# Two-stage weight conversion, a later GpSimd product, and other PSUM banks for the first and last batch

## The chip, the cores and the metric

The kernel runs on one core of a Trainium2 chip. The metric is the device time of one execution in microseconds (us). The engines are TensorE (PE; its weight loads are listed apart as PEld), VectorE (DVE), ScalarE (ACT), GpSimd (POOL), and SyncE (SP), which only issues DMAs here. Every engine works through its own queue in order.

## The reference, cut to what matters

Three blocks follow one another, for B = 8 batches, S = 576 tokens and width 512:

```python
# 1. retention: 8 heads of 64
scores = scale * q @ k.T
ret = scores * Dmat          # causal decay gamma ** (i - j)
x = (ret @ v)                # -> (B, S, 512)
# 2. four attention experts, two of them chosen per token
logits = x @ w_gate
for e in range(4):
    q, k, v = x @ wq[e], x @ wk[e], x @ wv[e]
    a = softmax(causal(scale * q @ k.T))
    out += weight_of_token_for_e * (a @ v @ wo[e])
# 3. mixing of tokens, then of channels
theta = x @ w_theta
zr, zi = x * cos(theta), x * sin(theta)
u = x + w_tok_r @ zr + w_tok_i @ zi
out = u + relu(u @ w_ch)
```

All inputs are float32. The weights of the third block reach the kernel as 64-bit floating-point numbers, seen as pairs of 32-bit words.

## The kernel before, in words

A large matmul is made of three: each operand is split into a high part and a low part (`split`, an ACT copy and a subtraction), and high by high, low by high and high by low are added in PSUM (`mm3`).

**First half, up to about 484 us.** Block 1 and block 2 are interleaved. A loop over 80 units (batch, pair of experts, row chunk) writes attention scores, transposes and products; a list of slots says in which unit a chunk of the next batch goes through retention (`ret_step`, a "visit") and which projections are made. The order on PE is the order of the code (`manual_schedule`); on the other engines a scheduler sets it, by its own estimate of when operands are ready. At a visit of chunk c, `ret_values` makes `xt`, ACT its high part `xh`, GpSimd its low part `xl` (L183), and the projections (L98 to L100, L242) then wait for both. The same visit loads chunk c+3 (`loads`: `kt` L114, `kv` L117) and has GpSimd multiply its values by decay factors (`vp`, L119). `vp` has three buffers, as have the loads.

Beside this, 51 jobs convert the 64-bit weights of block 3: a load (`raw`, L426), five operations on DVE (L433 to L439), an ACT copy of the low words (`r`, L441), GpSimd's `r*ex` (L442), an ACT copy for the high part (`h`, written to `hl`, L443), and GpSimd's `d = v-h` and `l = d+r` (L445, L446). All are written one behind the other in one job; the result goes back to DRAM with the next job (L453). The temporaries have one buffer each.

**Second half.** For each batch, `mix(b, h)` for h = 0, 1 (each 9 steps of contraction, two blocks of 128 channels, token columns in two pieces `TS` = 256 and 320) writes four PSUM banks `acc00` to `acc11`; DVE moves them to `u` (L723, for batch 0 L725), ACT and GpSimd or DVE split `u` (L726, L727). Then `channel` makes four blocks of 128 channels in the four banks named `w`, again in pieces of 256 and 320, and DVE evicts each (L740). The operands of `mix` come from `z_tile`: DVE takes |theta| (L564), subtracts pi/2 (L565), clamps (L566), ACT takes the sine of both halves at once (L567), DVE multiplies by x (L569), ACT and DVE split (L103, L104). `load_o` fetches attention outputs and token weights (`og`, one buffer, L519) and multiplies them on GpSimd (L520); `x_put` and `x_get` carry x, transposed by DVE (L751), through DRAM to the next batches' `u`.

Of the kernel before, what the change touches and what calls it, by code (L numbers as in the profile page):

```python
# [10 lines left out]
F32 = mybir.dt.float32  # L11
F32R = mybir.dt.float32r
# [48 lines left out]
def tile_kernel(ctx: ExitStack, tc: tile.TileContext, qk, kv, w1, wo, wot, wd, cst, out):  # L61
# [45 lines left out]
    MARK = {}  # L107
    QKT, KVT, XT, PSS, VP, SM, PX = {}, {}, {}, {}, {}, {}, {}

    def loads(b, c):  # L110
        R = ROWS[c]
        o = c * 1024
        t = ret.tile([128, 8, R], F32, name="kt", bufs=LDB, padded_shape=[128, 8, 128])
        nc.sync.dma_start(t, qk[b, :, o:o + 8 * R].rearrange("p (h r) -> p h r", h=8))  # L114
        n = R // 64
        u = ret.tile([128, 2, 2, 256], F32, name="kv", bufs=LDB)
        nc.sync.dma_start(u[:, :n], kv[b, c, :, :n * 512].rearrange("r (j a d) -> r j a d", j=n, a=2))  # L117
        vp = ret.tile([128, 2, 4, D], F32, name="vp", bufs=VPB)
        MARK["pool"] = nc.gpsimd.tensor_mul(vp[:, :n], u[:, :n, 1, :].rearrange("p j (h d) -> p j h d", h=4),  # L119
                                            gam[:, c, :n, :, None].to_broadcast([128, n, 4, D]))  # L120
        QKT[b, c], KVT[b, c], VP[b, c] = t, u, vp

# [300 lines left out]
    def convert(cvt, h, l, src, n):  # L423

        raw = cvt.tile([128, n, 2], I32, name="raw", bufs=2, padded_shape=[128, CV, 2])
        nc.sync.dma_start(raw, src.bitcast(I32).rearrange("p (n t) -> p n t", t=2))  # L426
        lo, hi = raw[:, :, 0], raw[:, :, 1]

        def tmp(name, dt):
            return cvt.tile([128, n], dt, name=name, bufs=1, padded_shape=[128, CV])  # L430

        b1 = tmp("b1", I32)
        nc.vector.tensor_scalar(b1, hi, 3, 0x3FFFFFF8, op0=OP.logical_shift_left, op1=OP.bitwise_and)  # L433
        nc.vector.scalar_tensor_tensor(b1, hi, -0x40000000, b1, op0=OP.bitwise_and, op1=OP.bitwise_or)
        ex = tmp("ex", I32)
        nc.vector.tensor_scalar(ex, hi, 0x7FF00000, None, op0=OP.bitwise_and)
        v = b1.bitcast(F32)
        nc.vector.scalar_tensor_tensor(v, ex, float(0x38100000), v, op0=OP.is_ge, op1=OP.mult)
        nc.vector.tensor_scalar(ex, b1, -0x800000, None, op0=OP.bitwise_and)  # L439
        r = tmp("r", F32)  # L440
        nc.scalar.activation(r, lo.bitcast(U32), AF.Copy, scale=2.0 ** -52)  # L441
        nc.gpsimd.tensor_mul(r, r, ex.bitcast(F32))  # L442
        nc.scalar.activation(h, v, AF.Copy)  # L443
        d = tmp("d", F32)
        nc.gpsimd.tensor_sub(d, v, h)  # L445
        nc.gpsimd.tensor_add(l, d, r)  # L446

    PEND = []

    def flush():  # L450
        while PEND:
            dst, t = PEND.pop()
            nc.sync.dma_start(dst, t)  # L453

    def cvt_jobs(pl, weights):

        def job(dst, off, o, n):
            t = pl.tile([128, 2, n], F32R, name="hl", bufs=2, padded_shape=[128, 2, CV])
            convert(pl, t[:, 0, :], t[:, 1, :], wd[:, off + o:off + o + n], n)
            flush()  # L460
            PEND.append((dst[:, :, o:o + n], t.bitcast(F32)))

        return [lambda a=(dst, off, x, min(CV, w - x)): job(*a) for dst, off, w in weights for x in range(0, w, CV)] + [flush]

# [48 lines left out]
    def load_o(b):  # L513
# [43 lines left out]
    def z_tile(g, i, h):  # L557
# [116 lines left out]
    def mix(b, h):  # L674
        g, w = divmod(b, 2)
        tiles = [0, 1, 2, 3, 4] if w == 0 else [4, 5, 6, 7, 8]
        acc = [[ps2.tile([128, t1 - t0], F32, name=f"acc{d}{i}", bufs=1, padded_shape=[128, 512])
                for i, (t0, t1) in enumerate(TS)] for d in range(2)]
        ks = []
# [48 lines left out]

    TAIL = {}

    def channel(b, et):
        uh, ul = UT[b]
        u = XU[b]
        es = slice(et * C, et * C + C)
        for t0, t1 in TS:
            ps = ps2.tile([128, t1 - t0], F32, name="w", bufs=4, padded_shape=[128, 512])
            for kt in range(4):
                mm3(ps, CH[:, kt, 0, es], CH[:, kt, 1, es], uh[:, kt, t0:t1], ul[:, kt, t0:t1], kt == 0, kt == 3)
            o = u[:, et, t0:t1]
            nc.vector.scalar_tensor_tensor(o, ps, 0.0, o, op0=OP.max, op1=OP.add)  # L740
            if b == B - 1:
# [31 lines left out]
    for b in range(B):  # L773
# [103 lines left out]
```

## Time and profile before

| | |
|---|---|
| median of 3 runs | 912.73 us (907.61 to 915.47) |
| profiled execution | 907.77 us, its span 905.8 us |
| busy in the span | PE 863.0 us (95%), PEld 803.9, DVE 628.8 (69%), ACT 454.9 (50%), POOL 218.9 (24%) |
| mean granted clock of TensorE | 0.992 |

A time is in us from the span's start. Matmuls are pipelined: the listed time of one is longer than the distance from its start to the next one's, and that distance is what a matmul costs PE. A number in square brackets at the end of a row is the idle time of the engine just before, with the instruction whose end released it.

### The profile page before, as it was taken

The numbers are of one execution on the slowest core, as the hardware profiler recorded it, in microseconds if no ns is written. First come the engines' busy times: TensorE is split into PE (matmuls) and PEld (weight loads), VectorE is DVE, ScalarE is ACT, GpSimd is POOL, SyncE is SP. The second block draws the span as 40 slices with busy tenths as digits, with TensorE's granted clock in tenths as the row PEclk, the third lists the DMA queues.
The fourth block names the chain that finished last, engine by engine and source line by source line (L and its number), as shares of the span: only waits on it lengthen the run. The fifth ranks groups of instructions, "written<-read, shape, count | busy, mean of one in ns | idle before, by whom it ended". The sixth has DMA issues, their size and how long they took to land.

```text
span 905.8 us, 25503 instructions
## 1 busy us (share of the span) xinstructions
PE 863.0 (95%) x10062; PEld 803.9 (89%) x10062; DVE 628.8 (69%) x1779; ACT 454.9 (50%) x1198; POOL 218.9 (24%) x268
## 2 busy tenths in 40 slices
PE   6998999899999999998999989999999999999998
PEld 6987888788898888888878889999999999999998
DVE  5376767878787776777769947866578764676732
ACT  2466666666666665665656513443244533434320
POOL 2434152452535434242212102001020110001010
PEclk8999999999999999999999999999999999999999
DMA  7857566676667667656795152333425123251401
GB/s 276 237 143 234 159 203 170 187 223 184 194 182 241 167 180 227 163 148 207 202 317 173 30 143 50 62 90 92 128 50 135 35 72 80 37 125 25 106 23 53
DMA packets 146216, 130.30 MB, mean 144 GB/s; under 512 B 83504, under 2 KB 121648, under 8 KB 146096
## 3 DMA queue, kind: packets, MB, share of 16 engines
q1 hardware_dynamic: 145952, 128.39, 50.1%
q8 instruction: 79, 1.29, 0.6%
q0 software_dynamic: 144, 0.28, 0.2%
q14 instruction: 41, 0.34, 0.1%
HBM read 78.03 MB, written 32.00 MB: 121 GB/s over the span
## 4 chain that ended last, share of the span: by engine, by line
PE 67%; DVE 10%; DMA 8%; ACT 6%; issue 3%; POOL 2%; SPq 2%; DVEq 0%; ACTq 0%; POOLq 0%
PE acc L711 22%; PE w L99 9%; PE w L98 9%; PE w L100 9%; PE w L242 4%; PE w L370 4%; PE w L304 3%; DMA kv<-kv 3%; PE w L351 2%; ACT P L312 2%; PE pS L150 2%; DVE P L307 1%; DMA TK<-td 1%; DMA wst<-w 1%; ACT U L225 1%
## 5 line engine op out<-in xcount | busy, mean ns | idle before, releaser
L711 PE MATMUL acc<-TK,zh 128*128 128x256 f32 (+1 forms) x1024 | 180.7, 299 | 3.4 <-ACT zh L103 1.8
L711 PEld LDWEIGHTS acc<-TK,zh 128*128 128x128 f32 x1024 | 155.7, 191 | 4.0 <-issue 3.7
L312 ACT ACTIVATE P<-P,st 128x128 f32<-128x128 f32 (+4 forms) x160 | 95.6, 598 | 55.9 <-DVE st L307 55.5
L711 PE MATMUL acc<-TK,zl 128*128 128x256 f32 (+1 forms) x512 | 110.9, 298 | 0.0
L727 POOL TENSOR_TENSOR ul<-u,uh 128x576 fp32r<-128x576 f32 x16 | 24.3, 1540 | 336.4 <-ACT uh L726 336.4
L307 DVE CUSTOM_DVE_ANT_0 P<-w,cm 128x128 f32<-128x128 f32 (+4 forms) x160 | 71.8, 477 | 24.4 <-PE w L304 24.1
L711 PEld LDWEIGHTS acc<-TK,zl 128*128 128x128 f32 x512 | 87.0, 191 | 0.0
L103 ACT ACTIVATE zh<-cs 128x512 fp32r<-128x512 f32 x64 | 40.4, 631 | 90.2 <-PE acc L711 68.2
L99 PE MATMUL w<-xl,WH 128*128 128x288 f32 x256 | 75.9, 296 | 4.5 <-POOL xl L183 4.5
L567 ACT ACTIVATE cs<-cs 128x512 f32<-128x512 f32 x72 | 45.2, 631 | 69.1 <-DVE cs L565 55.2
L98 PE MATMUL w<-uh,CH 128*128 128x256 f32 (+1 forms) x256 | 75.5, 297 | 2.4 <-ACT uh L726 2.4
L98 PE MATMUL w<-xh,WH 128*128 128x288 f32 x256 | 76.0, 297 | 0.7 <-ACT PT L356 0.7
L104 DVE TENSOR_TENSOR zl<-cs,zh 128x512 fp32r<-128x512 f32 x64 | 44.0, 690 | 46.4 <-ACT zh L103 45.7
L304 PE MATMUL w<-KK,U 128*64 128x288 f32 (+4 forms) x384 | 76.2, 327 | 0.0
L99 PE MATMUL w<-ul,CH 128*128 128x256 f32 (+1 forms) x256 | 75.7, 296 | 0.0
L100 PE MATMUL w<-uh,CH 128*128 128x256 f32 (+1 forms) x256 | 75.6, 296 | 0.0
L100 PE MATMUL w<-xh,WL 128*128 128x288 f32 x256 | 75.4, 295 | 0.0
L150 PE MATMUL pS<-vp,kv 64*64 64x64 f32 x1024 | 44.0, 226 | 19.8 <-ACT S L153 15.9
L442 POOL TENSOR_TENSOR r<-r,ex 128x192 f32<-128x192 f32 (+1 forms) x51 | 29.5, 579 | 136.4 <-ACT hl L443 61.8
L569 DVE SCALAR_TENSOR_TENSOR cs<-cs,x 128x512 f32<-128x512 f32 x72 | 48.7, 687 | 18.6 <-ACT cs L567 18.4
L304 PEld LDWEIGHTS w<-KK,U 128*128 128x128 f32 (+1 forms) x384 | 53.9, 171 | 7.5 <-issue 4.3
L150 PEld LDWEIGHTS pS<-vp,kv 64*64 64x64 f32 x1024 | 35.8, 137 | 27.1 <-ACT S L153 18.5
(140 smaller groups left out, 2267.2 us busy)
## 6 DMA issues: line engine op xcount, KB each, us to landing
KK<-KN SPq DMA_DIRECT2D x128, 144.0 KB
kt<-qk SPq DMA_DIRECT2D x32, 512.0 KB
kv<-kv SPq DMA_DIRECT2D x32, 512.0 KB
raw<-wd SPq DMA_DIRECT2D x43, 192.0 KB
xd<-xb SPq DMA_DIRECT2D x126, 64.0 KB
out<-u SPq DMA_DIRECT2D x28, 288.0 KB
u<-xd SPq DMA_DIRECT2D x28, 288.0 KB
td<-hl SPq DMA_DIRECT2D x27, 192.0 KB
```

The costliest lines, as they stand in the source:

```text
L98: nc.tensor.matmul(ps, ah, bh, start=first, stop=False)
L99: nc.tensor.matmul(ps, ah, bl, start=False, stop=False)
L100: nc.tensor.matmul(ps, al, bh, start=False, stop=last)
L103: nc.scalar.activation(h, src, AF.Copy)
L104: nc.vector.tensor_sub(l, src, h)
L150: nc.tensor.matmul(pS[half(s), x, :], u[half(s), j, 0, x * D:x * D + D], vp[half(s), j, x, :], start=k == 0 and x == 0, stop=False, skip_g ...
L304: nc.tensor.matmul(ps[s][:R], U[:, s, rs], KK[:, s, x, j0:j1], start=x == 0, stop=x == 1)
L307: MARK["dve"] = nc.vector.tensor_tensor_reduce(Ps[s][:R, j0:j1], ps[s][:R], cm[:R, o + j0:o + j1], 1.0, st[:R, 0, s:s + 1] if i else 3.0e3 ...
L312: MARK["act"] = nc.scalar.activation(Ps[s][:R, :n], Ps[s][:R, :n], AF.Exp, bias=st[:R, last, s:s + 1], scale=-1.0, accum_out=SUM[p][:R, m, ...
L567: nc.scalar.activation(cs, cs, AF.Sin)
L569: nc.vector.scalar_tensor_tensor(z, cs, -1.0, x2[:, None, ds].to_broadcast([128, 2, 256]), op0=OP.mult, op1=OP.mult)
L711: nc.tensor.matmul(acc[d][j], A[:, dc], TK[:, kt, W, t0:t1], start=q == 0 and n == 0, stop=q == 8 and n == 2)
```

## The change

1. **Conversion in two stages.** A job now first finishes the job before it (GpSimd's `r*ex`, ACT's `h`, GpSimd's `v-h`, in place, and the sum), and then does its own load, the five DVE operations and ACT's `r`. The temporaries have two buffers, and a result is stored one job later.
2. **GpSimd's product later.** `loads` only notes the chunk; `scale`, at the end of the next visit, makes `vp`.
3. **Banks for the edge batches.** For b = 0 and 7, `mix(b, 1)` accumulates in the four `w` banks, and `channel` of these batches in the `acc` banks.
4. **Pieces of 288.** Batches 1 to 7 in `mix` and all batches in `channel` use 288 and 288 columns for 256 and 320.
5. **pi/2 as a bias.** DVE's subtraction goes; ACT takes the sine in two instructions of 256, one with a bias.
6. **`load_o`'s product** waits for the last `channel` eviction written before it, if there is one.
7. **Batch 0's `x_put`s** are written behind the channel blocks, `x_get(1)` at the end.

```diff
     def loads(b, c):
...
-        vp = ret.tile([128, 2, 4, D], F32, name="vp", bufs=VPB)
-        MARK["pool"] = nc.gpsimd.tensor_mul(vp[:, :n], u[:, :n, 1, :].rearrange("p j (h d) -> p j h d", h=4),
-                                            gam[:, c, :n, :, None].to_broadcast([128, n, 4, D]))
-        QKT[b, c], KVT[b, c], VP[b, c] = t, u, vp
+        QKT[b, c], KVT[b, c] = t, u
+        RAW.append((b, c))
+
+    def scale_v(b, c):
+        n = ROWS[c] // 64
+        vp = VP[b, c] = ret.tile([128, 2, 4, D], F32, name="vp", bufs=VPB)
+        MARK["pool"] = nc.gpsimd.tensor_mul(vp[:, :n], KVT[b, c][:, :n, 1, :].rearrange("p j (h d) -> p j h d", h=4),
+                             gam[:, c, :n, :, None].to_broadcast([128, n, 4, D]))
+
+    def scale():
+        if RAW:
+            scale_v(*RAW.pop(0))
@@ -198,6 +209,8 @@
+        if (b, c) > (0, 1):
+            scale()
@@ -439,28 +455,42 @@
-        nc.gpsimd.tensor_mul(r, r, ex.bitcast(F32))
-        nc.scalar.activation(h, v, AF.Copy)
-        d = tmp("d", F32)
-        nc.gpsimd.tensor_sub(d, v, h)
-        nc.gpsimd.tensor_add(l, d, r)
...
+        def rest():
+            nc.gpsimd.tensor_mul(r, r, ex.bitcast(F32))
+            nc.scalar.activation(h(), v, AF.Copy)
+            nc.gpsimd.tensor_sub(v, v, h())
+            nc.gpsimd.tensor_add(l(), v, r)
...
+    def finish():
+        flush()
+        if REST:
+            rest, pl, n, dst = REST.pop()
+            t = pl.tile([128, 2, n], F32R, name="hl", bufs=2, padded_shape=[128, 2, CV])
+            HL[:] = [t]
+            rest()
+            PEND.append((dst, t.bitcast(F32)))
...
         def job(dst, off, o, n):
...
+            finish()
+            rest = convert(pl, lambda: HL[0][:, 0, :], lambda: HL[0][:, 1, :], wd[:, off + o:off + o + n], n)
+            REST.append((rest, pl, n, dst[:, :, o:o + n]))
@@ -517,7 +549,10 @@
-        nc.gpsimd.tensor_mul(OL[b], OL[b], gw)
+        m = nc.gpsimd.tensor_mul(OL[b], OL[b], gw)
+        if "ch" in MARK:
+            tc.add_manual_dep(m.ins, MARK["ch"].ins.name, mybir.DependencyInfo(
+                mybir.DependencyClass.Sync, mybir.DependencyReason.DATA), reason="behind the channel products")
@@ -562,9 +597,9 @@
-        nc.vector.tensor_scalar(cs[:, 0, :], cs[:, 0, :], math.pi / 2.0, None, op0=OP.subtract)
         nc.vector.tensor_scalar(cs[:, 1, :], nr[:, ds], PI_LO, -PI_LO, op0=OP.min, op1=OP.max)
-        nc.scalar.activation(cs, cs, AF.Sin)
+        nc.scalar.activation(cs[:, 0, :], cs[:, 0, :], AF.Sin, bias=quarter)
+        nc.scalar.activation(cs[:, 1, :], cs[:, 1, :], AF.Sin)
@@ -674,8 +709,10 @@
-        acc = [[ps2.tile([128, t1 - t0], F32, name=f"acc{d}{i}", bufs=1, padded_shape=[128, 512])
-                for i, (t0, t1) in enumerate(TS)] for d in range(2)]
+        ts = TH if b else TS
+        spare = h and b in EDGE
+        acc = [[ps2.tile([128, t1 - t0], F32, name="w" if spare else f"acc{d}{i}", bufs=4 if spare else 1,
+                         padded_shape=[128, 512]) for i, (t0, t1) in enumerate(ts)] for d in range(2)]
@@ -727,17 +764,20 @@
+    EDGE = (0, B - 1)
...
-        for t0, t1 in TS:
-            ps = ps2.tile([128, t1 - t0], F32, name="w", bufs=4, padded_shape=[128, 512])
+        for j, (t0, t1) in enumerate(TH):
+            spare = b in EDGE
+            ps = ps2.tile([128, t1 - t0], F32, name=f"acc{et % 2}{j}" if spare else "w", bufs=1 if spare else 4,
+                          padded_shape=[128, 512])
```

**How the order changes on GpSimd**, at the first visits of the second batch. `xl_1008` there is the low part of that batch; `kv_1015` is loaded at the visit that makes `xt_1009`. Before:

```order
29 L446 TENSOR_TENSOR hl_1039<-d_1053,r_1049 128x192
30 L119 TENSOR_TENSOR vp_1017<-kv_1015,gam_121 128x512
31 L183 TENSOR_TENSOR xl_1008<-xt_1009,xh_1007 128x4x128
32 L442 TENSOR_TENSOR r_1189<-r_1189,ex_1185 128x192
33 L445 TENSOR_TENSOR d_1193<-b1_1182,hl_1179 128x192
34 L446 TENSOR_TENSOR hl_1179<-d_1193,r_1189 128x192
```

After:

```order
27 L460 TENSOR_TENSOR r_1048<-r_1048,ex_1044 128x192
28 L127 TENSOR_TENSOR vp_1171<-kv_1015,gam_123 128x512
29 L194 TENSOR_TENSOR xl_1008<-xt_1009,xh_1007 128x4x128
30 L462 TENSOR_TENSOR b1_1041<-b1_1041,hl_1173 128x192
31 L460 TENSOR_TENSOR r_1187<-r_1187,ex_1183 128x192
32 L463 TENSOR_TENSOR hl_1173<-b1_1041,r_1048 128x192
```

The product of `kv_1015` still stands right ahead of the same `xl`; what moved is the conversion: a job's difference and sum now stand behind `xl`, with the next job's `r*ex` between them.

**On SyncE**, in the second batch, behind the small stores of token weights (`gd`). Before:

```order
33 L326 DMA gd_93<-nwt 5x2x32 x4
34 L114 DMA kt<-qk 128x8x64
35 L117 DMA kv<-kv 128x1024
36 L453 DMA tt_81<-hl 256x1x192
37 L117 DMA kv<-kv 128x1024
38 L114 DMA kt<-qk 128x1024
```

After:

```order
31 L339 DMA gd_93<-nwt 5x2x32 x4
32 L120 DMA kv<-kv 128x1024
33 L117 DMA kt<-qk 128x8x64
34 L472 DMA tt_81<-hl 256x1x192
35 L442 DMA raw<-wd 128x384
36 L120 DMA kv<-kv 128x1024
```

The first `kv` load has passed the `kt` load.

**On DVE**, where the first half ends. `nr_8921` before and `nr_8872` after read `pS`, a bank of the first half's PSUM pool, which must be free before `mix(0, 0)` can start. Before:

```order
1104 L550 TENSOR_SCALAR k_8877<-k_8877 128x512
1105 L552 TENSOR_TENSOR nr_8880<-k_8877,w_8868 128x512
1106 L104 TENSOR_TENSOR zl_8943<-cs_8936,zh_8942 128x512
1107 L569 SCALAR_TENSOR_TENSOR cs_8946<-cs_8946,x2_8563 128x512
1108 L550 TENSOR_SCALAR k_8918<-k_8918 128x512
1109 L564 TENSOR_SCALAR cs_8975<-nr_8609 128x256
1110 L552 TENSOR_TENSOR nr_8921<-k_8918,pS_8909 128x512
```

After:

```order
1102 L585 TENSOR_SCALAR k_8828<-k_8828 128x512
1103 L587 TENSOR_TENSOR nr_8831<-k_8828,w_8819 128x512
1104 L604 SCALAR_TENSOR_TENSOR cs_8887<-cs_8887,x2_8475 128x512
1105 L585 TENSOR_SCALAR k_8869<-k_8869 128x512
1106 L587 TENSOR_TENSOR nr_8872<-k_8869,pS_8860 128x512
1107 L107 TENSOR_TENSOR zl_8894<-cs_8887,zh_8893 128x512
```

The subtraction that frees the bank has moved ahead of a low part and of a second product of `z_tile`.

## Rows read from the trace of the kernel before

**Rows 1.** Waits of PE: who was waited for, us in total, times, longest.

```profile
PE pS L150 <- ACT S L153: 15.9, 19, 2.6
PE w L99 <- POOL xl L183: 4.5, 5, 1.9
...
PE w L242 <- POOL xl L183: 1.7, 1, 1.7
```

**Rows 2.** Timeline of SP and POOL, 133 to 144 us: start, duration, instruction.

```profile
133.06 3.35 SPq L220 DMA_DIRECT2D KK<-KN  x4
...
137.09 0.44 SPq L117 DMA_DIRECT2D kv<-kv  x1
...
143.23 1.04 POOL L119 TENSOR_TENSOR vp<-kv,gam 128x512 f32<-128x512 f32 x1 [3.11 <-DMA kv<-kv]
```

**Rows 3.** Timeline of SP and POOL, 67 to 74 us.

```profile
67.71 0.34 SPq L117 DMA_DIRECT2D kv<-kv  x1
...
73.46 1.04 POOL L119 TENSOR_TENSOR vp<-kv,gam 128x512 f32<-128x512 f32 x1 [6.04 <-DMA kv<-kv]
```

**Rows 4.** Timeline of DVE, ACT and PE, 176 to 180 us.

```profile
176.06 1.43 DVE L434 SCALAR_TENSOR_TENSOR b<-raw,b 128x192 int32<-128x192 int32 x1
...
177.92 0.36 ACT L443 ACTIVATE hl<-b 128x192 fp32r<-128x192 f32 x1 [1.26 <-DVE b L438]
...
178.86 0.39 ACT L153 ACTIVATE S<-pS 128x256 f32<-128x256 f32 x1
...
179.30 0.27 PE L150 MATMUL pS<-vp,kv 64*64 64x64 f32 x2 [2.12 <-ACT S L153]
```

**Rows 5.** Timeline of POOL, DVE and PE, 475 to 486 us.

```profile
475.01 2.68 POOL L520 TENSOR_TENSOR ol<-ol,og 128x1152 f32<-128x1152 f32 x1 [17.46 <-DMA og<-gd]
...
475.60 2.24 DVE L564 TENSOR_SCALAR cs<-nr 128x256 int32<-128x256 int32 x1
...
483.88 0.68 DVE L552 TENSOR_TENSOR nr<-k,pS 128x512 f32<-128x512 f32 x1
...
484.76 1.20 PE L711 MATMUL acc<-TK,zh 128*128 128x256 f32 x4 [1.79 <-ACT zh L103]
```

**Rows 6.** Busy time by stretch: stretch, its length, each engine, granted clock, DMA.

```profile
484.00:486.00 2.00, 1.24 (x6) 1.27 (x7) 2.00 (x7) 0.78 (x2) 0.00 (x0) 0.72 0.67 204
486.00:489.50 3.50, 3.50 (x20) 3.48 (x20) 3.19 (x7) 2.12 (x4) 0.00 (x0) 0.67 0.84 230
```

**Rows 7.** Timeline of DVE and PE, 491 to 524 us and near 874 us.

```profile
491.05 2.18 DVE L564 TENSOR_SCALAR cs<-nr 128x256 int32<-128x256 int32 x1
...
521.72 1.54 DVE L725 COPY u<-acc 128x256 f32<-128x256 f32 x4
...
503.91 0.47 PE L711 MATMUL acc<-TK,zh 128*128 128x256 f32 x2 [1.63 <-DVE u L725]
...
519.73 0.28 PE L98 MATMUL w<-uh,CH 128*128 128x256 f32 x1
...
523.30 0.39 PE L98 MATMUL w<-uh,CH 128*128 128x256 f32 x1 [2.40 <-ACT uh L726]
...
874.54 0.51 PE L711 MATMUL acc<-TK,zth 128*128 128x256 f32 x2 [1.52 <-DVE u L723]
```

**Rows 8.** Groups: DVE's in 485 to 521.7 us; ACT's of the whole span.

```profile
L565 DVE TENSOR_SCALAR cs<-cs 128x256 f32<-128x256 f32 x13 | 3.7, 285 | 0.0
...
L567 ACT ACTIVATE cs<-cs 128x512 f32<-128x512 f32 x72 | 45.2, 631 | 69.1 <-DVE cs L565 55.2
```

**Rows 9.** Timeline of PE: a stretch of `mix`, and one of projections.

```profile
760.31 0.70 PE L711 MATMUL acc<-TK,zh 128*128 128x256 f32 x4
...
764.31 0.70 PE L711 MATMUL acc<-TK,zh 128*128 128x256 f32 x4
...
76.36 0.29 PE L98 MATMUL w<-xh,WH 128*128 128x288 f32 x1
...
77.81 0.29 PE L100 MATMUL w<-xh,WL 128*128 128x288 f32 x1
```

More of the change, by code (lines that the diff above doesn't have):

```diff
@@ L33 @@
 TS = [(0, 256), (256, 576)]
+TH = [(0, 288), (288, 576)]
 CV = 192
@@ L82, in tile_kernel @@
     ident = consts.tile([128, 128], F32, name="ident")
+    quarter = consts.tile([128, 1], F32, name="quarter")
+    nc.vector.memset(quarter, -math.pi / 2.0)
     tri = att.tile([128, 64], F32, name="tri")
@@ L107, in tile_kernel @@
     MARK = {}
-    QKT, KVT, XT, PSS, VP, SM, PX = {}, {}, {}, {}, {}, {}, {}
+    QKT, KVT, XT, PSS, VP, SM, RAW = {}, {}, {}, {}, {}, {}, []
     def loads(b, c):
@@ L393, in tile_kernel @@
     loads(0, 0)
+    scale_v(0, 0)
     nc.sync.dma_start(tri, cst[:, 256:320])
     loads(0, 1)
+    scale_v(0, 1)
     o += NCH * H
@@ L416, in tile_kernel @@
         loads(0, c)
+        scale_v(0, c)
     with tc.issue_after(MARK["pool"].ins):
@@ L427, in convert, with tmp @@
         lo, hi = raw[:, :, 0], raw[:, :, 1]
-        def tmp(name, dt):
-            return cvt.tile([128, n], dt, name=name, bufs=1, padded_shape=[128, CV])
+        def tmp(name, dt, bufs=2):
+            return cvt.tile([128, n], dt, name=name, bufs=bufs, padded_shape=[128, CV])
         b1 = tmp("b1", I32)
@@ L441, in convert @@
         nc.scalar.activation(r, lo.bitcast(U32), AF.Copy, scale=2.0 ** -52)
-        nc.gpsimd.tensor_mul(r, r, ex.bitcast(F32))
-        nc.scalar.activation(h, v, AF.Copy)
-        d = tmp("d", F32)
-        nc.gpsimd.tensor_sub(d, v, h)
-        nc.gpsimd.tensor_add(l, d, r)
-    PEND = []
+        def rest():
[3 more added lines that the diff above has]
+            nc.gpsimd.tensor_add(l(), v, r)
+        return rest
+    PEND, REST = [], []
     def flush():
@@ L453, in flush @@
             nc.sync.dma_start(dst, t)
+    def finish():
[6 more added lines that the diff above has]
+            PEND.append((dst, t.bitcast(F32)))
+    HL = []
     def cvt_jobs(pl, weights):
         def job(dst, off, o, n):
[L458 to L463, printed above, removed]
+            finish()
+            rest = convert(pl, lambda: HL[0][:, 0, :], lambda: HL[0][:, 1, :], wd[:, off + o:off + o + n], n)
+            REST.append((rest, pl, n, dst[:, :, o:o + n]))
+        return [lambda a=(dst, off, x, min(CV, w - x)): job(*a) for dst, off, w in weights
+                for x in range(0, w, CV)] + [finish, flush]
     FW = []
@@ L500, in tile_kernel @@
         make_gt(c)
+    RAW[:3] = []
+    scale()
     w1s.release()
@@ L709, in mix @@
                 for n, (A, W) in enumerate(((zh, 0), (zh, 1), (zl, 0))):
-                    for j, (t0, t1) in enumerate(TS):
+                    for j, (t0, t1) in enumerate(ts):
                         nc.tensor.matmul(acc[d][j], A[:, dc], TK[:, kt, W, t0:t1], start=q == 0 and n == 0,
@@ L720, in mix @@
             k = 2 * h + d
-            for j, (t0, t1) in enumerate(TS):
+            for j, (t0, t1) in enumerate(ts):
                 if b:
@@ L739, in channel @@
             o = u[:, et, t0:t1]
-            nc.vector.scalar_tensor_tensor(o, ps, 0.0, o, op0=OP.max, op1=OP.add)
+            MARK["ch"] = nc.vector.scalar_tensor_tensor(o, ps, 0.0, o, op0=OP.max, op1=OP.add)
             if b == B - 1:
@@ L783, in tile_kernel @@
                 token_tile(ps2, *x)
-            x_put(*x)
+            if b:
+                x_put(*x)
         mix(b, 1)
@@ L788, in tile_kernel @@
                 token_tile(ps2, *x)
-            x_put(*x)
-        if b + 1 < B:
+            if b:
+                x_put(*x)
+        if 0 < b < B - 1:
             x_get(b + 1)
@@ L793, in tile_kernel @@
             channel(b, et)
+            for x in q[2 * et:2 * et + 2] if not b else []:
+                x_put(*x)
+        if not b:
+            x_get(1)
     ps2.release()
```

## The prediction, made before the changed kernel was run

> **What bounds the kernel now.** I read the page's busy times first: PE is busy for 863.0 of 905.8 us, so PE's 43 us of idle time, and what a matmul costs, are all there is to win. Next I listed the waits of PE, longest first. The largest total is `pS` waiting for ACT's copy of the state, 15.9 us in 19 waits, followed by `xl`, 4.5 + 1.7 = 6.2 us in six waits [rows 1]. Then I went through the timelines at each wait over 0.3 us, and asked which instruction ended last. In the second half PE stops only four times, at 484.76, 503.91, 523.30 and 874.54 [rows 5, 7]; between the last two there is no stop of that size, and there only a cheaper matmul can help. PE's instruction order in the first half is the same in both kernels, so there only waits can change.
>
> **The change part by part**, against the profiled execution (907.77 us, of which 905.8 is the span); gains with a minus.
>
> *Pieces of 288.* In `mix`, from 760.31 to 764.31 us stand 30 matmuls, 15 pairs of 256 + 320 columns: 4.00/15 = 0.2667 us a pair. In the projections, from 76.36 to 77.81 stand 11 steps of 288 columns: 1.45/11 = 0.1318 us, a pair 0.2636 [rows 9]. The change touches 7 batches x 108 pairs in `mix` and 8 x 48 in `channel`, 1140 pairs: 1140 x 0.0031 = **-3.5**. The projections change weights at each matmul, as `channel` does, while `mix` alternates two banks; so the other end is 0. I take -3.4, since the 288 row is the same shape.
>
> *Second half's banks.* `mix(0, 1)` waited 1.63 us for DVE to empty `acc`, `mix(7, 1)` 1.52 [rows 7]. The `w` banks are free then: batch 0's token tiles were all made in the first half, and batch 7 has none to make. **-3.1**; the other end is -2.6, if an operand of `zh` is a little late. The price is at the hand-over from `channel(0)`, now in `acc`, to `mix(1, 0)`: the last bank is evicted in about half a microsecond, and six matmuls of other banks (0.8 us) stand before it is wanted. I put 0 there.
>
> *DVE's queue in batch 0.* `channel(0)` starts at 519.73, but DVE gets to the four copies it needs only at 521.72: its queue is late. From the copies' start to the released matmul are 523.30 - 521.72 = 1.58 us. If DVE is on time, I take 0.4 us after 519.73, that matmul goes at 521.7; PE's other matmuls fill until 523.30 - 2.40 = 520.90, and 0.8 of the 2.40 us remain: **-1.6** (0 to -2.4) [rows 7]. Is DVE on time? It must win 1.6 us, and another 1.6 because `mix(0, 1)` starts sooner. It loses 13 subtractions (3.7 us busy, 2.6 at least by the distance of their starts) [rows 8], two low parts that belonged to batch 2, and the block at 491.05, 2.18 for an operation of as many elements as those of 0.285 [rows 7, 8]: 5 us or more. The five transposes of `x_put` stay among the `z_tile` operations by the scheduler's order, though they are written later; they are no gain.
>
> *The start of `mix(0, 0)`.* PE stopped 1.79 us until 484.76. The row names ACT's `zh`, but that had been ready; the last user of the old PSUM pool was DVE's `nr`, from 483.88 to 484.56 [rows 5]. It now stands ahead of two operations of about its own size, and the sine chain behind the 2.24 us block at 475.60 [rows 5] starts earlier as well, as GpSimd's product for batch 2 moves behind `channel(0)`. Next late is the copy of the last attention output on ACT; I take **-1.4** (0 to -1.8).
>
> The granted clock fell with that stop: 0.72 and 0.67 of full speed in the next two stretches, between 1.2 and 2.4 GHz [rows 6]. In 484.76 to 489.5 that costs about 0.28 x 1.24 + 0.33 x 3.50 = 1.5 us. The stops of 2.12 and 2.40 us elsewhere were followed by no such loss; PE had worked on small matmuls before this one. A shorter stop may not lower the clock: I take **-1.0** (0 to -1.5).
>
> The blocks are GpSimd's doing: its product ran from 475.01 to 477.69, and DVE's 2.24 us instruction ended at 477.84 [rows 5]. The Trainium skill, "SBUF — State Buffer", section "Who interferes with whom", says that the two share one pair of ports as an exclusive lock, and whoever issues second is blocked for the whole instruction; the row agrees. By that rule the product moved behind `channel(0)` blocks DVE there for up to its 2.7 us instead; without it, it would cost nothing there. The sum is the same either way, because PE has one `z_tile`'s worth of matmuls, 12 pairs or 3.2 us, between two things it wants of DVE at that place.
>
> *The later product.* I give it almost nothing by itself: GpSimd's queue still has the product of a load right ahead of the `xl` of the visit that issues the load, as the order shows. What changes is SP's queue. At 67.71 the `kv` load was issued behind a `kt` load, and `vp` waited 6.04 us for it until 73.46 [rows 3]; now it stands ahead of that `kt`, which gives some 0.4 us of issue and something of the transfer, against a stop of 1.7 us. The other five stops are of the last chunk of a batch: SP issued four `KK` copies from 133.06, then `kt`, then `kv` at 137.09, and `vp` had to wait until 143.23 [rows 2]. That is DMA work of some 1.6 MB in a row, not a late issue; the store of a converted weight ahead of it is ready about one GpSimd operation (0.6 us) sooner. Five times 0.3 to 0.6, and about 1.5: **-3.5** of the 6.2 (0 to -6.2) [rows 1].
>
> *Two-stage conversion.* At 179.30 PE waited 2.12 us for ACT's copy of the state, where such waits are 15.9/19 = 0.84 in the mean [rows 1]. ACT had been held by `h`, which waited 1.26 us for DVE's chain, itself blocked (1.43 us for one operation) [rows 4]. With `h` taken from the job before, ACT passes; next late is DVE's copy of transposes, behind that same chain, so I take about 0.8 of the 2.12 as won. One more such stop follows a batch later. **-1.5** for both (0 to -2.6); the other 17 waits for the state stay.
>
> *Costs.* 72 sine instructions become 144. One of 512 elements takes 0.63 us [rows 8], one of 192 of another function 0.36 [rows 4]: some 0.1 us each, 7 us on an engine that is half idle, and it shortens the chain by a DVE operation of 0.2 to 0.28. GpSimd's wait in `load_o` has `ul` of the next `mix` behind it, which is wanted only after that `mix`'s 18 steps. Batch 1's `u` is now partly loaded behind the last store of batch 0, still ahead of its use. All of this I put at 0. For waits that I don't see, from 51 jobs that stand a few places elsewhere, I add **+2**, two waits of the size of those in rows 1.
>
> Sum: -3.4 - 3.1 - 1.6 - 1.4 - 1.0 - 3.5 - 1.5 + 2 = **-13.5**, so 894.3 for the profiled execution. The three runs have their median 5 us above it, at 912.73; from there **899**.
>
> **The rivals.**
> 1. *The first half gains nothing.* `vp` stays ahead of `xl`, and the loads land when the DMA engines have moved them, not when they are issued. Without the 3.5 and 1.5: -8.5, **904**. For it: the unchanged order on GpSimd. Against: the `kv` load that passes `kt`.
> 2. *Two pieces of 288 cost what 256 + 320 do*, since a pair has the same 576 columns and two instructions in both. -10.1, **903**. For it: `mix` has two banks in turn, the projections one. Against: the 0.0031 us of the rows.
> 3. *Slower: GpSimd's queue is tied to the next job.* In 27 places the difference of the old job, `r*ex` of the new one, and the sum of the old one stand in this order, and in 22 of them a `vp` or `xl` is next or next but one. `r*ex` waits for the new job's load, DVE chain and ACT copy, so a late `raw` now holds up `xl`, and with it the projections. It decides once this comes later than ACT's `xh`. If 20 places cost PE 1.0 us each, as the six do now (6.2/6), it is +20 - 8.5: **924**. Against: the old order had the same wait for its own job, and PE's waits for `xl` came from `kv` alone.
>
> **How the numbers follow.** The forecast has 0.60, rival 1 0.22, rival 2 0.10, rival 3 0.06, and 0.02 is left for others. The range: below, every term near its favourable end, -19 from the fastest run, 889; above, only some -4 from the median, 909; it takes in the first two rivals, and 2 in 10 lie outside. A measurement of this kernel can tell about 1% from no change; that needs a time below 903.6. The forecast is below it in 8 of 10 cases, rivals 1 and 2 in about half: 0.48 + 0.16 = 0.64 for faster. Slower is rival 3: 0.06; the rest, 0.30, is within 1%.
>
> **What would show it.** The waits of PE should have no `acc` waiting for `u`, and `uh` at the start of `channel(0)` near 0.8; 576 columns in `mix` should take 0.264 us; the clock should stay at full speed at 484 us; PE's waits for `xl` should fall from 6.2 to about 2.7, and no wait for the state should be near 2 us. Waits of `xl` on conversions would prove rival 3. The prediction is wrong if the first half ends later than 483 us or if new stops appear between batches 1 and 7.

## The result, and the profile after

The changed kernel is slower by about 1.2%: 922.04 us in the median of 4 runs (917.69 to 924.30) against 911.06 of the kernel before, a ratio of 1.0115 [1.0082, 1.0148]. The profiled execution took 920.42 us (span 918.2), 12.7 more than the one of before. Two lines of its page, PE's busy time and its granted clock in 40 slices:

```profile
PE 871.1 (95%) x10062; PEld 811.2 (88%) x10062; DVE 622.6 (68%) x1708; ACT 465.8 (51%) x1270; POOL 220.8 (24%) x268
PEclk7999999999999999999999989999999999999999
```

PE is busy 8.1 us more than before with slightly cheaper matmuls, which points to its clock. To see where the time went, cut the span at two places that both kernels have. `mix(0, 0)` begins at 499.77 us instead of 484.76: the first half lost **15.0** us (the same matmul that went at 480 us before goes 16.3 us later; 1.3 came back at the start of `mix(0, 0)`). From there to the start of `mix(1, 0)` it takes 50.58 us, 50.43 before, and from there to the end of the span **2.8** us less.

The waits of PE, as in [rows 1] (who was waited for, us in total, times, longest):

```profile
PE pS L161 <- ACT S L164: 15.3, 19, 1.7
PE w L102 <- POOL xl L194: 11.2, 6, 2.6
...
PE acc L101 <- ACT uh L763: 3.3, 1, 3.3
```

The waits for `xl` are six in both kernels and have grown from 6.2 to 11.2 us in all. Behind four of them, and behind the stop at `channel(0)`, the clock is low. Stretches behind them (length, then PE, PEld, DVE, ACT, POOL; the third figure from the end is the granted clock):

```profile
90.00:95.00 5.00, 4.32 (x22) 4.30 (x23) 0.67 (x2) 0.41 (x1) 0.63 (x1) 0.66 0.04 14
148.00:153.00 5.00, 4.72 (x25) 4.71 (x26) 0.46 (x1) 0.41 (x2) 1.65 (x4) 0.66 0.06 15
206.00:211.00 5.00, 3.90 (x18) 3.89 (x19) 1.06 (x3) 0.51 (x2) 2.70 (x5) 0.66 0.00 1
320.00:324.00 4.00, 4.00 (x22) 3.98 (x22) 1.15 (x4) 0.41 (x1) 1.06 (x2) 0.57 0.02 6
536.00:541.00 5.00, 5.00 (x21) 5.00 (x22) 2.62 (x6) 1.39 (x3) 0.00 (x0) 0.50 0.00 0
```

The first four cost 3 x 5 x 0.34 + 4 x 0.43 = 6.8 us. So 5.0 us of longer `xl` waits and 6.8 us of clock make up 11.8 of the 15.0. The rest is not taken apart here; new stops of about 1 us stand in it, for `sm` (the masked scores of the retention, made by DVE), for `PT` (transposes, copied by DVE), for `KK` and for the state.

The first of the four is another case than the rest. The kernel before waited twice there, and the changed one, whose `kv` load has passed `kt`, once (before, before, after):

```profile
75.78 0.39 PE L242 MATMUL w<-WH,xl 128*128 128x260 f32 x1 [1.68 <-POOL xl L183]
90.84 0.40 PE L99 MATMUL w<-xl,WH 128*128 128x288 f32 x1 [0.99 <-POOL xl L183]
...
90.68 0.40 PE L102 MATMUL w<-xl,WH 128*128 128x288 f32 x1 [2.57 <-POOL xl L194]
```

The sum is nearly the same, 2.67 and 2.57 us. PE came earlier by what it had saved and waited for the next load instead; only behind the one longer stop was the clock low.

**How `xl` became late.** `KN` is a block of attention keys, and `KK` its four copies, which SyncE issues ahead of the visit's loads. The timelines of GpSimd, SyncE, DVE and PE in the visit of the second batch's last chunk:

```profile
133.22 0.60 POOL L462 TENSOR_TENSOR b<-b,hl 128x192 f32<-128x192 f32 x1 [2.42 <-ACT hl L461]
135.20 0.60 POOL L460 TENSOR_TENSOR r<-r,ex 128x192 f32<-128x192 f32 x1 [1.38 <-DVE ex L455]
135.75 0.60 POOL L463 TENSOR_TENSOR hl<-b,r 128x192 fp32r<-128x192 f32 x1
...
146.50 1.04 POOL L127 TENSOR_TENSOR vp<-kv,gam 128x512 f32<-128x512 f32 x1 [3.60 <-DMA kv<-kv]
147.50 0.72 POOL L194 TENSOR_TENSOR xl<-xt,xh 128x256 fp32r<-128x256 f32 x1
...
136.37 0.53 SPq L472 DMA_DIRECT2D tt<-hl  x1
136.99 3.11 SPq L233 DMA_DIRECT2D KK<-KN  x4
...
140.79 0.44 SPq L120 DMA_DIRECT2D kv<-kv  x1
...
135.30 0.45 DVE L107 TENSOR_TENSOR KN<-w,KN 128x288 fp32r<-128x288 f32 x1
...
148.28 0.40 PE L102 MATMUL w<-xl,WH 128*128 128x288 f32 x1 [2.60 <-POOL xl L194]
```

Read it from the top. The old job's difference is done at 133.82, but GpSimd's next instruction is the new job's `r*ex`, which waits 1.38 us for DVE; the old job's sum follows at 135.75. Its store waits in SyncE's queue until 136.37. `KN` was ready at 135.75, yet the `KK` copies go only at 136.99, 1.24 us later, and the `kv` load behind them at 140.79. `vp` waits for that load, `xl` stands behind `vp`, PE behind `xl`. In four of the six visits of a last chunk `KK` goes 1.24 to 1.38 us behind `KN`; in the kernel before it was 0.02 to 0.72 in five (and 1.69 in the first, where the changed kernel has 0.62). In the same visit before, `KN` was ready at 132.40 and `KK` went at 133.06 [rows 2]:

```profile
131.95 0.45 DVE L104 TENSOR_TENSOR KN<-w,KN 128x288 fp32r<-128x288 f32 x1
```

In two of the four late visits `r*ex` waits 1.38 us, as here. In the other two it does not wait and costs its own 0.55 us; there the old job's difference is itself late, behind ACT's `h`:

```profile
193.14 0.59 POOL L462 TENSOR_TENSOR b<-b,hl 128x192 f32<-128x192 f32 x1 [1.79 <-ACT hl L461]
193.69 0.59 POOL L460 TENSOR_TENSOR r<-r,ex 128x192 f32<-128x192 f32 x1
194.24 0.60 POOL L463 TENSOR_TENSOR hl<-b,r 128x192 fp32r<-128x192 f32 x1
```

It is the place of the wait that counts, not the total. SyncE waited for GpSimd's sums longer in the kernel before (49.1 us in 33 times) than in the changed one (27.7 in 23), but in three of the six visits before nothing held `KK`.

**A second way** lies where the two-stage job puts DVE's block at once behind its own load (DVE, ACT and PE):

```profile
172.91 0.26 DVE L449 TENSOR_SCALAR b<-raw 128x192 int32<-128x192 int32 x1 [2.31 <-DMA raw<-wd]
...
174.03 0.69 DVE L149 TENSOR_TENSOR sm<-w,tri 128x512 f32<-128x512 f32 x1
174.64 0.68 DVE L191 TENSOR_TENSOR xt<-w,gt 128x512 f32<-128x512 f32 x1
...
172.90 0.38 ACT L457 ACTIVATE r<-raw 128x192 f32<-128x192 uint32 x1 [2.16 <-DMA raw<-wd]
173.18 0.37 ACT L164 ACTIVATE S<-pS 128x256 f32<-128x256 f32 x1
...
174.78 0.48 PE L317 MATMUL w<-KK,U 128*64 128x288 f32 x2 [1.16 <-DVE sm L149]
```

DVE and ACT stand still for a load that is still under way, with `sm`, `xt` and the state's copy queued behind, and PE stops for `sm`. In the changed kernel DVE waited for `raw` five times, 6.4 us in all; in the kernel before never.

### The profile page after: what moved, and what is told of

It is laid out like the page before. It is cut to its first block, busy times and chain, and to the rows that moved or that the text cites. A ratio compares the mean times of both kernels' runs of the same rounds, so it can differ in the third digit from the quotient of the medians.

```text
span 918.2 us, 25431 instructions
## 1 busy us (share of the span) xinstructions
PE 871.1 (95%) x10062; PEld 811.2 (88%) x10062; DVE 622.6 (68%) x1708; ACT 465.8 (51%) x1270; POOL 220.8 (24%) x268
## 4 chain that ended last, share of the span: by engine, by line
PE 68%; DVE 8%; DMA 8%; issue 6%; ACT 4%; POOL 3%; SPq 2%; POOLq 0%; ACTq 0%; DVEq 0%
PE acc L748 22%; PE w L102 8%; PE w L103 8%; PE w L101 8%; PE w L255 4%; PE w L383 3%; PE w L317 3%; DMA kv<-kv 3%; PE pS L161 2%; PE w L364 2%; PE w L748 2%; ACT P L325 2%; POOL xl L194 1%; PE acc L101 1%; PE acc L103 1%
## 5 line engine op out<-in xcount | busy, mean ns | idle before, releaser
L748 PE MATMUL acc<-TK,zh 128*128 128x288 f32 (+2 forms) x896 | 155.9, 296 | 0.5 <-ACT ob L387 0.5
L748 PEld LDWEIGHTS acc<-TK,zh 128*128 128x128 f32 x896 | 131.9, 189 | 0.8 <-issue 0.6
L748 PE MATMUL acc<-TK,zl 128*128 128x288 f32 (+1 forms) x448 | 95.8, 295 | 0.0
L102 PE MATMUL w<-xl,WH 128*128 128x288 f32 x256 | 77.2, 302 | 11.2 <-POOL xl L194 11.2
L748 PEld LDWEIGHTS acc<-TK,zl 128*128 128x128 f32 x448 | 72.4, 189 | 0.0
L601 ACT ACTIVATE cs<-cs,quarter 128x256 f32<-128x256 f32 x72 | 36.4, 506 | 60.0 <-DVE cs L599 60.0
L161 PE MATMUL pS<-vp,kv 64*64 64x64 f32 x1024 | 45.1, 229 | 19.8 <-ACT S L164 15.3
L604 DVE SCALAR_TENSOR_TENSOR cs<-cs,x 128x512 f32<-128x512 f32 x72 | 49.3, 688 | 19.2 <-ACT cs L602 18.4
L462 POOL TENSOR_TENSOR b<-b,hl 128x192 f32<-128x192 f32 (+1 forms) x51 | 31.3, 613 | 128.8 <-ACT hl L461 118.7
L127 POOL TENSOR_TENSOR vp<-kv,gam 128x512 f32<-128x512 f32 (+1 forms) x40 | 38.5, 964 | 95.7 <-DMA kv<-kv 73.5
L102 PEld LDWEIGHTS w<-xl,WH 128*128 128x128 f32 x256 | 49.3, 193 | 13.2 <-POOL xl L194 12.6
L383 PE MATMUL w<-PT,V 128*64 128x192 f32 (+3 forms) x576 | 55.9, 324 | 4.3 <-DVE PT L369 3.4
```

Of the source, the lines that this page charges most:

```text
L102: nc.tensor.matmul(ps, ah, bl, start=False, stop=False)
L161: nc.tensor.matmul(pS[half(s), x, :], u[half(s), j, 0, x * D:x * D + D], vp[half(s), j, x, :], start=k == 0 and x == 0, stop=False, skip_g ...
L383: nc.tensor.matmul(po[s * 64:s * 64 + 64, c0:], V[:ROWS[j], j, 2 * p + s, :], v, start=j == 0, stop=j == last, skip_group_check=True)
L604: nc.vector.scalar_tensor_tensor(z, cs, -1.0, x2[:, None, ds].to_broadcast([128, 2, 256]), op0=OP.mult, op1=OP.mult)
```

## The experiments

All medians are beside runs of the kernel before on the same chip (908.6 to 911.1 us). The changed kernel's own was 911.06, the others' 908.6 to 909.6, so a difference between its median and a run's is uncertain by some 2 us or more. The column "m" is the start of `mix(0, 0)` in the profiled run, "xl" PE's waits for `xl`, both in us.

| run | median | ratio to before | m | xl |
|---|---|---|---|---|
| changed kernel | 922.0 | 1.0115 [1.0082, 1.0148] | 499.8 | 11.2 |
| e1_sum_first | 911.9 | 1.0050 [1.0031, 1.0069] | 491.4 | 6.4 |
| e2_xl_first | 899.4 | 0.9904 [0.9880, 0.9928] | 478.4 | 0 |
| e3_one_stage | 904.3 | 0.9942 [0.9913, 0.9972] | 483.8 | 5.2 |
| e4_256_320 | 919.5 | 1.0118 [1.0075, 1.0161] | 499.8 | 11.8 |
| e5_before_two_stage | 924.6 | 1.0178 [1.0140, 1.0217] | 500.9 | 11.4 |
| e6_before_xl_first | 900.3 | 0.9906 [0.9878, 0.9934] | 478.0 | 0 |
| e7_u_first | 892.8 | 0.9824 [0.9795, 0.9852] | 479.1 | 0 |
| e8_xl_first_one_stage | 895.2 | 0.9853 [0.9827, 0.9878] | 477.0 | 0 |
| e9_load_ahead | 909.1 | 1.0000 [0.9973, 1.0027] | 488.1 | 8.0 |
| e10_u_first_one_stage | 888.0 | 0.9750 [0.9705, 0.9795] | 473.5 | 0 |
| e11_u_first_load_ahead | 892.1 | 0.9790 [0.9748, 0.9832] | 475.2 | 0 |
| e12_u_first_one_stage_load_ahead | 888.0 | 0.9746 [0.9709, 0.9783] | 473.8 | 0 |
| e13_store_pool | 903.6 | 0.9946 [0.9920, 0.9972] | 491.7 | 9.6 |
| e14_sum_first_load_ahead | 905.8 | 0.9958 [0.9926, 0.9989] | 486.9 | 7.5 |

**e1: the old sum first.**

```diff
-            nc.gpsimd.tensor_mul(r, r, ex.bitcast(F32))
+            m = nc.gpsimd.tensor_mul(r, r, ex.bitcast(F32))
+            if "sum" in MARK:
+                behind(m, MARK["sum"])
...
+            MARK["sum"] = nc.gpsimd.tensor_add(l(), v, r)
```

> The changed kernel with one edge more: GpSimd's product r*ex of a job stands behind the sum of the job before. This swaps 27 pairs on GpSimd and moves nothing on any other engine. Theory A (the store chain): in the changed kernel the sum of an old job waits behind r*ex of the next one (1.38 us idle at 135.2), its store waits in SP's queue until 136.37, and the four KK copies and the kv load behind it come about 1 us later against PE, so vp and behind it xl are late, PE stops for 2.5 us and its clock falls. Then PE's waits for xl, 11.3 us in the last chunks' visits of the changed kernel, fall to about 5 to 6, the four clock falls of some 1.5 us each go, and the first half (until mix(0, 0) starts) ends near 488 instead of 499.8; the time is 908 to 912. Theory B (the conversions lie elsewhere, the order of GpSimd does not matter): xl waits stay near 11 us, the first half ends at 498 to 501, the time stays at 920 to 924.

The numbers are near theory A's: 911.9, `xl` at 6.4, one fall of the clock instead of four. But the first half ended at 491.4, not 488: the `sm` waits stayed, and PE's waits for the state came to 18.1 us (15.3 in the changed kernel), with stops of 1.5 to 1.7. The order of two instructions on an engine that is 24% busy is worth 8.4 us in the first half of the profiled runs (10 between the medians, 6 by the two ratios). The two visits where the difference waits for ACT are not cured: `KK` still goes 0.9 us behind `KN` there.

**e2: `xl` ahead of `vp`.**

```diff
+        XLI[b, c] = MARK.get("xl")
...
+            k = RAW.pop(0)
+            scale_v(*k)
+            behind(MARK["pool"], XLI[k])
```

> The changed kernel with vp of a load placed behind the xl of the visit that issues the load (an added edge on GpSimd; PE, DVE and ACT keep their order). If PE's long stops come from xl standing behind a vp that waits for kv, whatever made kv late, all of the xl waits go (11.3 us to under 1), with them the clock falls (about 6 us): the first half ends near 483 to 485, the time is 905 to 908. If the stops come from xh or from other GpSimd work (r*ex waiting for the next job's load), xl waits stay above 6 us and the time stays over 915.

Better than expected. GpSimd's timeline now has `xl` first, waiting only for ACT, and `vp` finds its load landed:

```profile
139.16 0.74 POOL L203 TENSOR_TENSOR xl<-xt,xh 128x256 fp32r<-128x256 f32 x1 [1.20 <-ACT xh L202]
139.98 1.11 POOL L132 TENSOR_TENSOR vp<-kv,gam 128x512 f32<-128x512 f32 x1
```

Part 2 of the change writes `vp` behind `xl`; without an edge the scheduler put it in front again.

**e3: one stage again**, the rest of the change kept (`convert` and the jobs of the kernel before).

> The changed kernel with the conversion of the kernel before (one stage, one buffer for each temporary); the rest of the change stays. If the two-stage conversion is what costs the first half its 15 us, the first half ends at 483 to 487 and the time is 904 to 909 (the second half's gains stay, its loss of about 5.5 us at channel(0) too). If the later product or another part of the change costs it, the first half still ends at 495 or later and the time stays over 916.

First half and time are both within the first range: without the two-stage conversion the 15 us are gone.

**e4: pieces of 256 and 320** (`TH = [(0, 256), (256, 576)]`).

> The changed kernel with pieces of 256 and 320 columns in place of 288 and 288 everywhere. If pieces of 288 are cheaper by 0.0031 us a pair, as the rows of before gave, mix and channel together take 3.4 us longer than in the changed kernel (mix(1) to the end: 371.3 in place of 367.9). If two pieces cost what their columns cost, mix and channel change by under 0.8 us. The first half and the stop at channel(0) are the same in both.

From `mix(1, 0)` to the last matmul PE takes 365.1 us against 364.1 with pieces of 288: 1.0 us, near the second case (under 0.8) and far from the first (3.4).

**e5: the two-stage conversion alone, on the kernel before.**

> The kernel before with the two-stage conversion alone. If the conversion by itself costs the first half what the changed kernel lost there, mix(0, 0) starts at 497 to 501 in place of 484.8, PE's waits for xl are 9 us or more with two or more falls of the clock, and the time is 920 to 926. If it costs that only together with the later product (GpSimd or SP order), mix(0, 0) starts before 490 and the time is under 915.

The first half ends at 500.9 and the time is 924.6: both as in the changed kernel, so the loss needs no other part of the change.

**e6: `xl` ahead of `vp`, alone, on the kernel before.**

> The kernel before with vp of a load placed behind the xl of the visit that issues the load, nothing else. If the six waits for xl (6.2 us) are all due to that order, they go and mix(0, 0) starts at 477 to 480, the time is 901 to 904. If xl then waits for something else on GpSimd (a conversion's product), less than 3 us are gained.

All six waits go, `mix(0, 0)` starts at 478.0, and the time is 900.3, although a stop of 4.1 us for `u` is new in the second half.

**e7: `u` first.** The edge in `z_tile`, on top of e2:

```diff
+        if (g, h) == (0, 0) and i > 5:
+            behind(m, MARK["u0"])
```

Here `m` is the first DVE operation of a tile and `u0` the last copy of `u` in `mix(0, 1)`.

> e2_xl_first with DVE's operations for three of the operand tiles of mix(1, 0) placed behind the four copies of u that channel(0) waits for. If the stop at channel(0) (3.6 us in e2_xl_first, and 1.7 us of clock behind it) is DVE's queue, it falls to 0.8 to 1.2 us, the clock stays up, channel(0) takes 14 us instead of 18 and the time is 4 to 4.5 us below e2_xl_first's 899.4, at 895. If the copies then wait on something else, or the moved operations stop mix(1, 0), the gain is under 1.5 us.

The gain is 6.6 us, more than expected. DVE waits for PE at the end of `mix(0, 1)` instead of the reverse, and no stop over 0.2 us is left at `channel(0)`. The block takes 12.9 us instead of 18.1 (the copies on DVE, the first matmul of the block on PE and one behind where the stop was):

```profile
509.88 1.62 DVE L773 COPY u<-w 128x256 f32<-128x256 f32 x4 [0.86 <-PE w L759]
...
510.62 0.30 PE L101 MATMUL acc<-uh,CH 128*128 128x288 f32 x1
...
511.84 0.29 PE L102 MATMUL acc<-ul,CH 128*128 128x288 f32 x1
```

**e8: e2 with one stage.**

> e2_xl_first with the conversion of the kernel before. If the two-stage conversion costs only by way of the xl wait, the first half ends at 477 to 480 as in e2_xl_first (478.4) and the time is 898 to 901. If it costs by itself as well (its new stops at 168 to 175 and its longer waits for the state), one stage is 3 to 6 us faster: mix(0, 0) at 473 to 475, 894 to 896. If its own gain counts (the two waits for the state of 2 us that it removed), one stage is 2 to 4 us slower.

In time it is the second case (895.2), in the first half the first (477.0): the profiled run shows 1.4 of the 4.2 us there. That run had a fall of the clock at 420 us (1.7 us); between 160 and 410 us of its time e2 loses 5.0 us against it, at stops for `sm`, for `PT` and for the state.

**e9: the load one job earlier.** `raw` of job i + 1 is loaded by job i; GpSimd and DVE keep their order.

```diff
             finish()
+            load(i)
+            load(i + 1)
-            rest = convert(pl, lambda: HL[0][:, 0, :], lambda: HL[0][:, 1, :], wd[:, off + o:off + o + n], n)
+            rest = convert(pl, lambda: HL[0][:, 0, :], lambda: HL[0][:, 1, :], raws[i], n)
```

> The changed kernel with the load raw of each job issued one job earlier; the order on GpSimd and DVE stays that of the changed kernel, SP's alike but for the place of raw. If the root is that DVE, ACT and GpSimd stand in their queues waiting for a raw that the same job has just issued (2.31 us on DVE at 172.91 with sm and xt behind, 1.38 us on GpSimd at 135.20 with the sum of the old job behind, and its store ahead of KK and kv in SP's queue), both go: the waits for sm disappear, xl waits fall from 11.3 to 5 to 7 us, mix(0, 0) starts at 484 to 488, the time is 905 to 910. If the order r*ex before the old sum costs through DVE's chain or ACT's copy and not through raw, xl waits stay at 9 us or more and the time over 916.

The time is 909.1, within the first range, and the first half ends at 488.1, at its edge; DVE's waits for `raw` fall to 0.7 us at the longest. `xl` stayed over the range (8.0). The old sum still stands behind `r*ex`, but that is not all of it: e14 below puts the sum first as well and still has 7.5.

**e13 and e14: the two ways apart, and together.** e13 issues the stores of converted weights on GpSimd (`nc.gpsimd.dma_start(dst, t)`), e14 joins e1 and e9.

> The changed kernel with the stores of converted weights issued by GpSimd behind the sum instead of by SyncE. PE, DVE and ACT keep their order but for a few rows. If the sum's lateness costs through SyncE's queue (the store waits there, and the KK copies and the kv load behind it), KK is issued within 0.1 us of KN in the last chunks' visits where the changed kernel has 1.2 to 1.4 us, xl waits fall from 11.3 to 6 or 7 us, mix(0, 0) starts at 489 to 493, as with the sum first (491.4). If GpSimd's order costs directly, by xl standing behind the late sum, xl waits stay over 9 us and mix(0, 0) starts after 496.

> The changed kernel with both: the old sum ahead of the next r*ex, and the load raw one job earlier. If these two are the ways in which the two-stage conversion costs the first half its 16 us (sum first alone gave 8.4, load ahead alone 11.6, partly the same), mix(0, 0) starts at 482.5 to 486, as with one stage (483.8), and the time is 903 to 907. If a third cost stays, it starts at 487 or later, no better than with the load ahead alone (488.1).

In e13 `KK` goes 0.03 us behind `KN` in all six visits; in the visit shown above, `KN` (DVE) and what SyncE then issues:

```profile
131.33 0.45 DVE L107 TENSOR_TENSOR KN<-w,KN 128x288 fp32r<-128x288 f32 x1
...
131.80 3.55 SPq L233 DMA_DIRECT2D KK<-KN  x4
...
136.04 0.45 SPq L120 DMA_DIRECT2D kv<-kv  x1
```

The median of ten runs is 903.6, 18 us below the changed kernel (15 by the ratios) with `r*ex` still ahead of the old sum. In two of the visits (189 and 245 us) the sum ends 0.7 us behind `KN`, and `KK` no longer waits for it; in the one shown, `r*ex` itself no longer waits. So the late sum held `KK` by way of SyncE's queue. How much of the 18 us that is, is not shown: e13 also spares SyncE the issue of 51 stores, some 0.55 us each, and the kernel before was not run with its stores moved. The profiled run was the slowest of the ten (910.44), and its `xl` waits (9.6) missed the range, on the side of the second case; there `kv` took 4.7 to 6.9 us from the end of its issue to `vp` (4.6 to 5.8 in the changed kernel), for a reason that stays open. e14 gives 905.8, 1.5 us from one stage, but 486.9 in the first half, between the two cases. One visit still had a wait of 2.8 us for `xl`: there the difference waited 1.76 us for ACT's `h`, so the sum and its store were late although the sum stood first, and `KK` went 1.46 us behind `KN`.

**e10 to e12: towards a faster kernel**, e7 with one stage, with the load ahead, and with both.

> e7_u_first with the conversion of the kernel before. The one-stage conversion was 4 us faster with xl first (895.2 against 899.4), 1.4 of them in the first half of the profiled runs; the two edits touch different halves, so they should add: 888.5 to 891.5, with no stop over 1 us at channel(0).

> e7_u_first (xl first, u first, two stages) with the load raw one job earlier. The stops of PE for sm (1.1 to 1.4 us at 166 and 327 us in e2_xl_first) came from DVE's wait for raw: if so they go, and the time is 3 to 5 us below e7_u_first's 892.8, at 888 to 890. If they come from DVE's queue being full, the time stays within 1.5 us of 892.8.

> e10_u_first_one_stage with the load raw one job earlier. In one stage the scheduler puts DVE's block behind other work until raw is there, so little waits for raw: within 2 us of e10_u_first_one_stage. If DVE waits for raw there too, it is 2 to 4 us faster than e10.

e10 is 888.0, just below its range and 2.5% faster than the kernel before, and its clock is at nine tenths or more in every slice but the first:

```profile
PE 858.7 (97%) x10062; PEld 800.5 (90%) x10062; DVE 614.8 (69%) x1708; ACT 469.3 (53%) x1270; POOL 221.2 (25%) x268
...
PEclk8999999999999999999999999999999999999999
```

The load ahead adds nothing to one stage (e12), as expected; with two stages the `sm` waits shrink by 0.8 to 0.9 us each, but the median by only 0.7 (e11), less than expected. In no pair of runs was the conversion in two stages faster than in one.

## Why the prediction was wrong

*What failed first* is the pair of terms for the first half: **-3.5** for `xl` and **-1.5** for the two stages, which came to +15.0 with the clock. The step behind both was "With `h` taken from the job before, ACT passes". It does: the stops of 2.12 us [rows 4] and 1.66 for the state are gone, though new ones (1.61 us at 179.52) leave the total at 15.3 us, after 15.9. But the job was cut behind DVE's block, so the block and ACT's `r` came up next to a load just issued, and GpSimd's `r*ex` ahead of the old sum. I counted that edit's instructions and not what they wait for. e3 and e5 show that the two stages cost the 15 us, with and without the rest of the change; e1 and e13 show the one way, e9 the other.

*Rival 3* named the pattern (difference, `r*ex`, sum) and the sign, and its 924 is 2 us off; I gave it 0.06. That it comes so near is partly luck: it has +20 - 8.5, where the profiles have +15.0 and -2.6. Its path was wrong as well: in the late visits `xl` does not wait for the sum on GpSimd. The sum holds a store, the store holds `KK` and `kv` on SyncE (e13). [rows 2] showed the four `KK` copies ahead of `kv`, and I took that time as DMA work, "not a late issue"; what stood ahead of `KK` was the thing to ask. My ground against it, "the old order had the same wait for its own job", misses that the old scheduler placed that block late, when `raw` had landed.

*The clock* had a term in one place only, -1.0 at `mix(0, 0)`, and there it was right (1.7 us gained; the clock is 1.00 from 484 to 530 us). That a stop elsewhere costs nothing, taken from stops of 2.12 and 2.40 us, did not hold for new ones of 1.75 to 3.33 us, five of which were followed by 1.7 to 2.8 us of loss.

*DVE's queue* (-1.6) was mis-sized: from the start of `mix(0, 0)` to the second copies DVE gained 2.4 us (34.54 against 36.96) where I counted 5 or more, and PE arrives 3.4 us earlier. The stop grew from 2.40 to 3.33 us, with 5.5 us at half clock behind it (2.75). e7 shows that DVE's order makes the stop.

```profile
531.34 0.30 PE L101 MATMUL acc<-uh,CH 128*128 128x288 f32 x1
...
535.89 0.61 PE L101 MATMUL acc<-uh,CH 128*128 128x288 f32 x1 [3.33 <-ACT uh L763]
...
534.31 1.54 DVE L762 COPY u<-w 128x256 f32<-128x256 f32 x4
```

*Pieces of 288* (-3.4): about -1.0, rival 2 (0.10). The projections of [rows 9] were the wrong neighbour. In `mix` itself, 30 matmuls of 288 columns:

```profile
773.93 0.69 PE L748 MATMUL acc<-TK,zh 128*128 128x288 f32 x4
...
777.94 0.69 PE L748 MATMUL acc<-TK,zh 128*128 128x288 f32 x4
```

4.01/15 = 0.2673 us a pair, against 0.2667 before. `channel` gains a little, 12.71 against 12.79 us.

*Right*: the edge banks (-3.1): `mix(0, 1)` and `mix(7, 1)` start without a stop, 1.6 and 1.8 us. The start of `mix(0, 0)` (-1.4): 1.79 us became 0.49. The later product as such gave next to nothing, as rival 1 had it: e3's first half is 1.0 us shorter than that of the kernel before, no more than the start of `mix(0, 0)`, and its `xl` waits are 5.2 us after 6.2. `load_o`'s product behind `channel(0)` blocked nothing: it ran from 551.09 to 553.76 us, where DVE had nothing else to run. The sine in two instructions takes 0.91 us in place of 0.63, three times the added 0.1 us that I put down ([rows 4] and [rows 8] give 0.2), but no wait of PE shows it.

```profile
499.77 0.88 PE L748 MATMUL acc<-TK,zh 128*128 128x256 f32 x5 [0.49 <-ACT ob L387]
```

Left open: how the 15 us divide between the two ways and ACT's late `h`, since e1 (10.2 us between the medians), e9 (13.0) and e13 (18.4) overlap; what e13's move would be worth without a late sum; and why `kv` landed late in e13's profiled run.

## What to carry to other kernels

When a job is cut in two, cut it between the load and the first instruction that reads it: what stands next to its own load waits in order, with everyone else's work behind it. Even so, ask whether it needs cutting: with the load ahead, two stages stayed slower than one here (909.1 and 904.3 us, e9 and e3; 892.1 and 888.0, e11 and e10). Follow a late result through the queue that stores it, SyncE's above all: the store holds back unrelated loads, and these may be what PE waits for. And where a scheduler sets the order, a line written later is not an instruction placed later; only an edge made it so, and that one edge was worth 8 us by itself (e6).

## What the runs showed of the hardware that I had not expected

Stops of PE of 1.75 to 2.6 us were followed by some 3 to 4 us in which the granted clock was at half, as the four stretches above show, though stops of 1.68, 1.90 and 2.12 us in the kernel before were not. Behind the last two of these the clock was full:

```profile
145.00:150.00 5.00, 4.99 (x41) 4.99 (x42) 2.02 (x9) 1.54 (x5) 0.00 (x0) 1.00 0.18 42
179.00:184.00 5.00, 4.70 (x71) 4.18 (x72) 1.74 (x7) 2.82 (x9) 2.93 (x4) 1.00 1.03 325
```

So a stop of some 2 us can cost 1.7 us more than itself. Its length alone does not decide it. In e13 a stop of 1.88 us was followed by a low clock, and a longer one of 2.82 us was not:

```profile
144.36 0.40 PE L102 MATMUL w<-xl,WH 128*128 128x288 f32 x1 [1.88 <-POOL xl L194]
201.59 0.40 PE L102 MATMUL w<-xl,WH 128*128 128x288 f32 x1 [2.82 <-POOL xl L194]
...
144.00:149.00 5.00, 4.64 (x25) 4.63 (x26) 1.90 (x6) 0.41 (x1) 2.36 (x5) 0.66 0.13 37
201.50:206.50 5.00, 4.91 (x40) 4.91 (x41) 1.72 (x8) 1.54 (x5) 2.38 (x5) 1.00 0.29 78
```

And two matmuls of 288 columns into two banks in turn took as long as 256 and 320 (0.2673 and 0.2667 us).
